# Transfers with more distance in the attention, maxima sent by ScalarE, and another order of row differences at the joint, in a transformer block on one core

## Chip, core and metric

The kernel runs on one core of one Trainium2 chip, in one launch. The metric is the device time of that launch in microseconds (us); lower is better. The engines are TensorE (PE; its weight loads are PEld), VectorE (DVE), ScalarE (ACT), GpSimd (POOL) and SyncE (SP), whose only work here is to issue DMA transfers, one after the other.

## What is computed

One transformer block of 2048 rows and width 512, modulated by a condition vector. The attention has 32 heads of 16 and four segments of 512 rows: causal attention inside a segment, mixed by a gate with a read of a memory of the segments before. A dense layer with gelu follows.

```python
h = _layernorm(x) * (1 + ca) + sa
x = x + ga * attention(h)              # 32 heads, 4 segments of 512 rows
h = _layernorm(x) * (1 + cb) + sb
x = x + gb * (gelu(h @ w1 + b1) @ w2 + b2)

# attention, for one segment s
p = softmax(qs @ ks.T * scale + causal_mask)
a_mem = (phi(qs) @ M) / (phi(qs) @ z + 1e-6)
o = g * a_mem + (1 - g) * (p @ vs)     # then o @ wo
M, z = M + phi(ks).T @ vs, z + phi(ks).sum(rows)
```

## The kernel before

There are four stages. The first (0 to about 200 us) projects q, k and v of all segments and reads the memory. The attention follows (about 200 to 486 us). Then comes the dense layer: its first product in fourteen "quads" (`quad`), which combine two row halves and two column halves with seven products in place of eight, each of them from high and low parts in three matmuls, and its second product (`ffn2`). The joint is the passage from the attention to the first quads.

**The attention.** P counts pairs of heads (0 to 63), Q groups of four heads of one segment (0 to 31), U groups of eight (0 to 15). For each Q, `load_stacks` loads a stack of q and one of k (qst, kst; four buffers of each), which hold each value as several bf16 terms in 96 rows. `s_part` (places S) computes the logits with rows on partitions only to take their maxima: `masked_max` (L613) does that with the causal mask on VectorE; for the two narrower blocks TensorE adds the mask as a product (L645) and one `tensor_reduce` takes the maxima of two heads (L617). `m_rows` (L661, GpSimd) splits the maxima into three bf16 terms, `m_put` turns them by a product (L667) and ScalarE copies them to a tile ms, and `m_send` (L675) stores them as rows 96 to 98 of the q stack. `st_part` (places T) then computes the logits transposed, with the maxima already subtracted (L693); ScalarE takes the exponential (L708, L719), and GpSimd's `affine_select` (L696) clears what is above the diagonal. `pv_part` (L733) multiplies by the values and a column of ones, which gives the denominators.

After that a U goes through memory: `pv_out` copies the result (ScalarE), `pv_store` stores it to TD (L751), `pv_in` loads the denominators dn and the values opk (L756, L758), the memory's share amB (L765) and for the last segment its divisor rm (L770, multiplied by `mem_mix`, L800). `den` inverts dn (VectorE, GpSimd), `den_store` stores it to RD (L784), `rb_in` loads it back spread over the rows, rbB (L788). `mix` multiplies and adds (L793, L795; GpSimd for U under 13), and `o_hi` (ScalarE) and `o_lo` make high and low parts. `wo_part` (L821) projects them, `wo_out` adds the rows of x, and `wo_store` stores the result to X2D (L847). Of the finished segments `ln2_load` loads the rows xt back (L556), `ln2_stats`, `ln2_rstd` and `ln2_apply` (L568; GpSimd for segment 0) normalise them, and `ln2_turn` (L574, L576) transposes them for the dense layer.

**What sets the order.** The order on each engine is written out by hand. `ap(place, f, ...)` puts a step at a place; one Q is 20 places, so Q's own products run at 20 Q to 20 Q + 20. ORDER says where among a step's S and T parts the places c0 to c19 lie. The dictionary PRM holds the distances: `dnl` (pv_in behind the last PV product), `den`, `rbl` (rb_in behind den), `rdl` (den_store behind den), `mix`, `ohi`, `olo` relative to 40 U; `mrows`, `mput`, `msl` for the maxima; `ln` and `ht` for the segments' normalisation and transposes. A transfer issued by SP waits in its turn for everything that it needs, and those behind it wait with it. At the joint, what is still left of the places is called by name with `rest(U, ...)`. There `r_sub` builds the row differences t1 to t4 from the transposed rows hr, `r_hi` (ScalarE) and `r_lo` (VectorE) make their high and low parts, and `w_hi` and `w_lo` those of w1. In the quads `bg(n, i, f, ...)` puts a background step into part i of quad n; `g_out` (L1085) applies gelu to a part and stores it (GD, L1086); `ln2_load3` loads the rows of segment 3.

Of the kernel before, what the change touches and what calls it, by code (L numbers as in the profile page):

```python
# [33 lines left out]
 'den': [84, 84, 84, 84],  # L34
 'dnl': 11,
 'rbl': 12,
 'rdl': 4,
 'tsl': 4,
 'msl': 2,
 'xol': 6,  # L40
 'mix': 107,
 'ohi': 117,
 'olo': 119,
 'end': {'rbl': 7, 'mix': 103, 'ohi': 111, 'olo': 116},
 'wo': [[20 * i + o for i in range(8) for o in (2, 5)]] * 2 + [[20 * i + o for i in range(4) for o in (2, 5, 8, 14)]],
 'wox': -25,
 'olate': 16,
 'mixu': 13,
 'olou': 13,
 'ht': [493, 503, 513, 523],  # L50
 'ht1': 644,
 'ln': [[400, 413, 449, 454], [531, 566, 603, 624]],
 'lnl': [0, 4, 20, 34],
# [23 lines left out]
 'mmix': 88,  # L77
 'lnd': [[11, 10], [10, 2]],
# [3 lines left out]
 'm': [0, 0, 0, 1],  # L82
# [19 lines left out]
def block_kernel(ctx: ExitStack, tc: tile.TileContext, x, wq, wk, wv, wo, betaq, betam,  # L102
                 w1, b1c, w2, b2, ccol, wmod, maskbd, mask8, out):
    nc = tc.nc
    v, act, pool, pe, sp = nc.vector, nc.scalar, nc.gpsimd, nc.tensor, nc.sync
# [57 lines left out]
    NK = 4  # L163
# [420 lines left out]
    with ExitStack() as pb:  # L584
# [89 lines left out]
        def m_send(Q):  # L674
            sp.dma_start(qst[Q % NK][96:99], mss.pop(Q))  # L675
# [255 lines left out]
        def ap(pos, f, *a):  # L931
            at(pos // 10, pos % 10, f, *a)
# [20 lines left out]
        for U in range(16):  # L953
            z = U // 4
            ap(40 * U + 20 + PRM["pv"][3][0] + PRM["dnl"], pv_in, U)
            if U == 15:
                ap(40 * U + 20 + PRM["pv"][3][0] + PRM["dnl"], am_in, U)
            p = {**PRM, **PRM["end"]} if U > 13 else PRM
            den_at = 40 * U + PRM["den"][z]
            ap(den_at, den, U)  # L960
            if U < 14:
                ap(den_at + PRM["rdl"], den_store, U)
            ap(den_at + p["rbl"] + (5 if U == 14 else 0), rb_in, U)
            assert 20 + PRM["pv"][3][0] + PRM["dnl"] <= PRM["den"][z] and PRM["den"][z] + p["rbl"] <= p["mix"]
            ap(40 * U + PRM["mmix"], mem_mix, U)
            ap(40 * U + p["mix"], mix, U)
            assert PRM["mmix"] <= p["mix"]
            late_by = PRM["olate"] if U in (6, 10) else 0
            ap(40 * U + p["ohi"] + late_by, o_hi, U)
            ap(40 * U + p["olo"] + late_by, o_lo, U)  # L970
            assert PRM["den"][z] <= p["mix"] <= p["ohi"] <= p["olo"]
# [12 lines left out]
        for i, (ln, ld) in enumerate(zip(PRM["ln"], PRM["lnd"])):  # L984
            assert ln[0] + PRM["lnl"][3] * i > 160 * i + 241 + PRM["wo"][i][15] and ln[1] > ln[0]
            assert ln[1] + 3 * ld[0] < ln[2] < ln[3] and ln[3] + 3 * ld[1] < (PRM["ht"][0], PRM["ht1"])[i]
        assert PRM["ln"][1][0] > PRM["ht"][3] and PRM["ht"] == sorted(PRM["ht"])
# [9 lines left out]
        for i, (ln, ld) in enumerate(zip(PRM["ln"], PRM["lnd"])):  # L997
# [43 lines left out]
    with ExitStack() as pc:  # L1041
# [134 lines left out]
        rest(15, "mem_mix")  # L1176
        r_lo(0, "t1")
        r_lo(0, "t2")
# [52 lines left out]
        bg(2, 1, ln2_load3)  # L1231
# [196 lines left out]
```

## Time and profile before

| | |
|---|---|
| median of 3 runs | 810.78 us (809.48 to 811.25) |
| profiled execution, its own time | 808.31 us |
| its span, first to last instruction | 806.6 us |
| busy: PE, DVE, ACT, POOL | 778.6, 553.5, 476.2, 331.8 us |
| mean granted TensorE clock | 0.992 |
| moved by DMA | 156.09 MB, mean 194 GB/s |

Times within the profile are microseconds from the first instruction. An entry of the timeline reads: start, duration, engine, line, operation, output tile, input tiles, shapes, count, and in brackets the idle time of the engine before it with what ended it. "SPq" and "ACTq" are the queues in which an engine issues its transfers. An entry of the waits reads: who waits, for whom, us in total, number of times, longest. Matmuls are pipelined, so from one to the next the starts count and not the durations.

### The profile page before, as it was taken

To read this page: it belongs to the slowest core of one execution; us is meant where nothing else is said; L and a number is where in the kernel's file an instruction comes from. 1 tells how busy PE (TensorE), PEld (TensorE's weight loads), DVE (VectorE), ACT (ScalarE), POOL (GpSimd) and SP (SyncE) were. 2 spreads that over 40 slices of the span, in tenths; PEclk is the share of its full clock that TensorE was granted. 3 is DMA by queue.
4 is the path that set the end of the run, shared out by engine and by line. 5 is a ranking of instruction groups with operands and counts; after the bars stand their busy time and mean duration, and the time that the engine had idled before them with its cause. 6 is when DMAs were issued, how large, how long until landed. Compare 5 with 4: busy or idle time off the path is not lost.

```text
span 806.6 us, 14065 instructions
## 1 busy us (share of the span) xinstructions
PE 778.6 (97%) x4631; PEld 539.2 (67%) x4631; DVE 553.5 (69%) x1275; ACT 476.2 (59%) x910; POOL 331.8 (41%) x554
## 2 busy tenths in 40 slices
PE   8999999999999999998989798989999999999998
PEld 4877767876545455554545455768888888888887
DVE  6686697458888877876867687867668866632523
ACT  4465545465888877775777475757745336653221
POOL 1347266451578655565875485133000404400000
PEclk9999999999999999999999999899999999999999
DMA  9596857395555667767657764585575744445443
GB/s 338 179 320 230 277 181 238 142 328 175 169 165 164 189 191 197 194 174 224 173 173 200 196 175 135 166 266 170 203 252 165 221 135 154 161 143 165 157 136 117
DMA packets 108817, 156.09 MB, mean 194 GB/s; under 512 B 16324, under 2 KB 55620, under 8 KB 108744
## 3 DMA queue, kind: packets, MB, share of 16 engines
q1 hardware_dynamic: 107880, 153.63, 60.9%
q10 hardware_dynamic: 864, 1.57, 0.5%
q8 instruction: 36, 0.59, 0.3%
q14 instruction: 37, 0.30, 0.1%
HBM read 93.95 MB, written 60.83 MB: 192 GB/s over the span
## 4 chain that ended last, share of the span: by engine, by line
PE 74%; DMA 7%; DVE 6%; ACT 4%; POOL 4%; issue 3%; SPq 1%; ACTq 0%; DVEq 0%; POOLq 0%
PE bx L1080 8%; PE att L693 7%; PE pv L733 7%; PE q L313 5%; PE bx L1345 5%; PE att L606 5%; PE by L1345 4%; PE bv L1345 4%; PE k L313 4%; PE bv L1080 4%; PE mm L821 3%; PE v L464 3%; PE spare L1345 2%; PE by L1080 2%; DMA qst<-ms 2%
## 5 line engine op out<-in xcount | busy, mean ns | idle before, releaser
L613 DVE CUSTOM_DVE_ANT_0 dump<-att,maskb 128x512 bf16<-128x512 f32 (+1 forms) x292 | 159.4, 595 | 44.6 <-PE att L606 22.0
L708 ACT ACTIVATE pt<-att 128x384 f32<-128x384 f32 (+1 forms) x256 | 124.8, 544 | 24.6 <-PE att L693 21.2
L696 POOL TENSOR_SCALAR_AFFINE_SELECT pt<-pt 128x256 f32<-128x256 f32 x256 | 103.2, 421 | 74.3 <-ACT pt L708 59.3
L693 PE MATMUL att<-qst,kst 99*128 99x256 bf16 (+3 forms) x512 | 108.3, 302 | 7.6 <-DMA qst<-ms 5.7
L693 PEld LDWEIGHTS <-kst 99*128 99x128 bf16 x512 | 43.8, 98 | 71.8 <-issue 35.9
L865 POOL TENSOR_TENSOR wb<-wa 128x256 f32<-128x256 f32 x24 | 21.4, 894 | 154.9 <-DMA wa<-in_w 144.3
L606 PE MATMUL att<-kst,qst 96*128 96x512 bf16 (+1 forms) x292 | 76.5, 344 | 3.9 <-DMA qst<-QD 3.3
L733 PE MATMUL pv<-pt,V 128*32 128x512 f32 (+1 forms) x992 | 79.6, 439 | 0.0
L719 ACT ACTIVATE pt<-att 128x256 f32<-128x256 f32 (+1 forms) x128 | 62.7, 493 | 23.2 <-PE att L693 22.7
L617 DVE TENSOR_REDUCE nm<-att 128x2 f32<-128x256 f32 (+1 forms) x110 | 56.4, 534 | 15.0 <-PE att L645 11.6
L136 DVE TENSOR_TENSOR gl<-s,gh 128x512 fp32r<-128x512 f32 x34 | 23.7, 697 | 42.1 <-ACT gh L133 42.1
L733 PEld LDWEIGHTS pv<-pt,V 128*32 128x32 f32 x992 | 25.9, 109 | 36.2 <-issue 28.1
L133 ACT ACTIVATE gh<-s 128x512 fp32r<-128x512 f32 x34 | 21.3, 628 | 46.3 <-PE spare L1345 16.7
L1085 ACT ACTIVATE s<-s,b1t 128x512 f32<-128x512 f32 x42 | 30.2, 720 | 17.9 <-DVE s L1089 17.9
L1089 DVE TENSOR_TENSOR s<-bv,s 128x512 f32<-128x512 f32 x28 | 19.2, 687 | 24.4 <-PE bv L1080 19.0
L606 PEld LDWEIGHTS <-qst 96*128 96x128 bf16 x292 | 23.7, 98 | 13.6 <-issue 7.6
L509 POOL TENSOR_TENSOR q<-qr,q 128x512 bf16<-128x512 f32 x16 | 18.7, 1168 | 27.8 <-ACT q L508 27.5
L645 PE MATMUL att<-maskb,identb 128*128 128x256 bf16 x110 | 29.9, 278 | 0.0
L500 POOL TENSOR_SCALAR qp<-qp 128x512 f32<-128x512 f32 x12 | 18.8, 1563 | 25.8 <-ACT qp L495 25.8
L136 DVE TENSOR_TENSOR w1ml<-s,w1mh 128x512 fp32r<-128x512 f32 x18 | 13.0, 721 | 22.5 <-ACT w1mh L133 22.5
L643 PE MATMUL att<-kst,qst 96*128 96x128 bf16 (+1 forms) x110 | 27.3, 248 | 0.8 <-ACT pt L708 0.8
L133 ACT ACTIVATE w1mh<-s 128x512 fp32r<-128x512 f32 x18 | 11.3, 629 | 26.8 <-PE spare L1345 11.3
(364 smaller groups left out, 2152.0 us busy)
## 6 DMA issues: line engine op xcount, KB each, us to landing
GD<-s SPq DMA_DIRECT2D x56, 256.0 KB
s<-GD SPq DMA_DIRECT2D x52, 256.0 KB
kst<-KD SPq DMA_DIRECT2D x32, 384.0 KB
qst<-QD SPq DMA_DIRECT2D x32, 384.0 KB
TD<-ts SPq DMA_DIRECT2D x32, 256.0 KB
xt<-X2D SPq DMA_DIRECT2D x28, 256.0 KB
wa<-in_w SPq DMA_DIRECT2D x28, 256.0 KB
QD<-q SPq DMA_DIRECT2D x16, 384.0 KB
```

Of the source, the lines that this page charges most:

```text
L136: lo_eng.tensor_tensor(out=lo, in0=src, in1=hi.bitcast(F32), op=ALU.subtract)
L313: pe.matmul(ps, a[:, k, 128 * g:128 * g + 128], b[k], start=(k == 0 and i == 0), stop=(k == KB - 1 and i == 2))
L606: pe.matmul(ps, q_of(P, h, i), k_of(P, h, 128 * (i + 1)), start=True, stop=True)
L613: v.tensor_tensor_reduce(out=dump[n_dump[0] % 2][:, :n], in0=src, in1=maskb[:, 512 - n:], scale=-1.0, scalar=-4 * NEG, op0=ALU.add, op1=AL ...
L617: v.tensor_reduce(out=dst, in_=src, axis=AX.X, op=ALU.max, negate=True)
L693: pe.matmul(ps, k[:99, e, 128 * j:128 * j + 128], q[:99, e, 128 * j:512], start=True, stop=True)
L696: pool.affine_select(out=t, in_=t, pattern=pattern, compare_op=ALU.is_ge, fill=0.0, base=0, channel_multiplier=-1)
L708: act.activation(pt[:, h, :], ps[:, :n], AF.Exp, scale=0.25)
L719: act.activation(pt, pv_, AF.Exp, scale=0.25)
L733: pe.matmul(ps[32 * c:32 * c + 32, lo:hi], V[4 * s + j][:, VW * hd:VW * hd + 32], pt[:, c % 2, lo - o:hi - o], start=start, stop=stop)
L1080: pe.matmul(ps, a[:, i, k, :], b[k], start=start and k == 0 and c == 0, stop=k == 1 and c == 2, skip_group_check=not start)
L1345: pe.matmul(ps, a[:, c], w[:, lo:hi], start=(f == 0 and i == 0), stop=(last and i == 2))
```

## The change

- In the attention the places of `pv_in`, `den`, `rb_in`, `mix`, `o_hi` and `o_lo` are later for U 0 to 10 and 12; U 11 and 13 ("quick") keep the old ones, 14 and 15 ("end") too. `mem_mix` of U 12 goes from 88 to 100. The delay of the high and low parts of U 6 and 10 (`olate`) is dropped.
- `m_send` of Q 10 to 31 is issued by ScalarE's queue in place of SP's.
- From Q 14 on, one more of the narrow maxima (first pair of the Q, 256 columns) is taken with the mask on VectorE, so its mask product goes.
- The loads, statistics and applications of segments 0 and 1 have places of their own; the transposes of segment 0 move from 493, 503, 513 to 498, 506, 514.
- At the joint all row differences are VectorE's, and the order of differences, high and low parts and the last denominators is another.
- The rows of segment 3 are loaded in part 2 of quad 3 in place of part 1 of quad 2.

```diff
--- before.py
+++ after.py
@@ -31,26 +31,27 @@
  'mrows': -21,
  'mput': -13,
  'stacks': -65,
- 'den': [84, 84, 84, 84],
- 'dnl': 11,
- 'rbl': 12,
+ 'den': 92,
+ 'dnl': 18,
+ 'rbl': 18,
  'rdl': 4,
  'tsl': 4,
  'msl': 2,
+ 'msa': 10,
  'xol': 6,
- 'mix': 107,
- 'ohi': 117,
- 'olo': 119,
- 'end': {'rbl': 7, 'mix': 103, 'ohi': 111, 'olo': 116},
+ 'mix': 120,
+ 'ohi': 130,
+ 'olo': 132,
+ 'quick': {'dnl': 11, 'den': 84, 'rbl': 12, 'mix': 107, 'ohi': 117, 'olo': 119},
+ 'end': {'dnl': 11, 'den': 84, 'rbl': 7, 'mix': 103, 'ohi': 111, 'olo': 116},
  'wo': [[20 * i + o for i in range(8) for o in (2, 5)]] * 2 + [[20 * i + o for i in range(4) for o in (2, 5, 8, 14)]],
  'wox': -25,
- 'olate': 16,
  'mixu': 13,
  'olou': 13,
- 'ht': [493, 503, 513, 523],
+ 'ht': [498, 506, 514, 523],
  'ht1': 644,
- 'ln': [[400, 413, 449, 454], [531, 566, 603, 624]],
- 'lnl': [0, 4, 20, 34],
+ 'ln': [{'in': [388, 397, 408, 417], 'stat': [420, 427, 434, 446], 'rstd': 449, 'on': [460, 467, 481, 487]},
+        {'in': [528, 537, 548, 568], 'stat': [566, 576, 586, 596], 'rstd': 603, 'on': [624, 626, 628, 630]}],
  'wl': [26, 66, 80, 81],
  'gate': 197,
  'vb': [1, 0, 1, 0],
@@ -74,12 +75,11 @@
  're': 'v',
  'am3': 1,
  'rme': 'p',
- 'mmix': 88,
- 'lnd': [[11, 10], [10, 2]],
+ 'mmix': 100,
  'mp': 0,
  'wout': ['vvvv', 'vava', 'vvvv'],
  'dens': ['p', 'p', 'p', 'v'],
- 'm': [0, 0, 0, 1],
+ 'm': [0, 1, 0, 1],
  'mq': 14,
  'pvo': ['a', 'a'],
  'mse': 'a',
@@ -672,7 +672,7 @@
         mss = {}
 
         def m_send(Q):
-            sp.dma_start(qst[Q % NK][96:99], mss.pop(Q))
+            (sp if Q < PRM["msa"] else act).dma_start(qst[Q % NK][96:99], mss.pop(Q))
 
         pts = {}
         late = []
@@ -952,23 +952,22 @@
                 ap(20 * Q + pvo + PRM["tsl"], pv_store, Q)
         for U in range(16):
             z = U // 4
-            ap(40 * U + 20 + PRM["pv"][3][0] + PRM["dnl"], pv_in, U)
+            p = {**PRM, **(PRM["end"] if U > 13 else PRM["quick"] if U in (11, 13) else {})}
+            in_at, den_at = 40 * U + 20 + PRM["pv"][3][0] + p["dnl"], 40 * U + p["den"]
+            ap(in_at, pv_in, U)
             if U == 15:
-                ap(40 * U + 20 + PRM["pv"][3][0] + PRM["dnl"], am_in, U)
-            p = {**PRM, **PRM["end"]} if U > 13 else PRM
-            den_at = 40 * U + PRM["den"][z]
+                ap(in_at, am_in, U)
             ap(den_at, den, U)
             if U < 14:
                 ap(den_at + PRM["rdl"], den_store, U)
             ap(den_at + p["rbl"] + (5 if U == 14 else 0), rb_in, U)
-            assert 20 + PRM["pv"][3][0] + PRM["dnl"] <= PRM["den"][z] and PRM["den"][z] + p["rbl"] <= p["mix"]
-            ap(40 * U + PRM["mmix"], mem_mix, U)
+            assert in_at <= den_at and p["den"] + p["rbl"] <= p["mix"]
+            mm_at = 88 if p["mix"] < 120 else PRM["mmix"]
+            ap(40 * U + mm_at, mem_mix, U)
             ap(40 * U + p["mix"], mix, U)
-            assert PRM["mmix"] <= p["mix"]
-            late_by = PRM["olate"] if U in (6, 10) else 0
-            ap(40 * U + p["ohi"] + late_by, o_hi, U)
-            ap(40 * U + p["olo"] + late_by, o_lo, U)
-            assert PRM["den"][z] <= p["mix"] <= p["ohi"] <= p["olo"]
+            assert mm_at <= p["mix"] <= p["ohi"] <= p["olo"]
+            ap(40 * U + p["ohi"], o_hi, U)
+            ap(40 * U + p["olo"], o_lo, U)
         for s in range(NSEG - 1):
             for b in range(4):
                 w = [160 * s + 240 + i for i in PRM["wo"][s][4 * b:4 * b + 4]]
...
@@ -994,12 +994,12 @@
         at(-1, 9, swap)
 
         ap(PRM["gate"], gate_load)
-        for i, (ln, ld) in enumerate(zip(PRM["ln"], PRM["lnd"])):
+        for i, ln in enumerate(PRM["ln"]):
             for b in range(4):
-                ap(ln[0] + PRM["lnl"][b] * i, ln2_load, i, b)
-                ap(ln[1] + ld[0] * b, ln2_stats, i, b)
-                ap(ln[3] + ld[1] * b, ln2_apply, i, b, (pool, v)[i])
-            ap(ln[2], ln2_rstd, i)
+                ap(ln["in"][b], ln2_load, i, b)
+                ap(ln["stat"][b], ln2_stats, i, b)
+                ap(ln["on"][b], ln2_apply, i, b, (pool, v)[i])
+            ap(ln["rstd"], ln2_rstd, i)
         for j in range(2):
             for i in range(4):
                 ap(PRM["wsub"][j] + i, w_sub, j, i, v)
@@ -1161,21 +1161,21 @@
         rest(15, "pv_in", "am_in")
         for b in range(4):
             wo_seg(3, b, range(2))
-        for i in range(2):
-            w_hi(0, i)
-        w_lo(0, 0)
+        w_hi(0, 0)
         r_sub(0, "t1")
         r_hi(0, "t1")
+        w_lo(0, 0)
         r_sub(0, "t2")
+        w_hi(0, 1)
+        r_lo(0, "t1")
         r_hi(0, "t2")
         w_lo(0, 1)
         rest(15, "den", "rb_in")
         rest(14, "mem_mix")
+        r_lo(0, "t2")
+        rest(15, "mem_mix")
         for n in ("t3", "t4"):
-            r_sub(0, n, pool)
-        rest(15, "mem_mix")
-        r_lo(0, "t1")
-        r_lo(0, "t2")
+            r_sub(0, n)
         rest(14, "mix")
         for b in range(4):
             wo_x(3, b)
@@ -1228,7 +1228,7 @@
             for b in range(lo, hi):
                 ln2_apply(s, b, v)
 
-        bg(2, 1, ln2_load3)
+        bg(3, 2, ln2_load3)
         for s, n in ((2, 2), (3, 4)):
             for b in range(4):
                 bg(n, 1 + b, ln2_stats, s, b)
```

More of the change, by code (lines that the diff above doesn't have):

```diff
@@ L983, in block_kernel @@
         assert PRM["wl"] == sorted(PRM["wl"]) and PRM["gate"] > PRM["wl"][1] + 60
-        for i, (ln, ld) in enumerate(zip(PRM["ln"], PRM["lnd"])):
-            assert ln[0] + PRM["lnl"][3] * i > 160 * i + 241 + PRM["wo"][i][15] and ln[1] > ln[0]
-            assert ln[1] + 3 * ld[0] < ln[2] < ln[3] and ln[3] + 3 * ld[1] < (PRM["ht"][0], PRM["ht1"])[i]
-        assert PRM["ln"][1][0] > PRM["ht"][3] and PRM["ht"] == sorted(PRM["ht"])
+        for i, ln in enumerate(PRM["ln"]):
+            assert all(a > 160 * i + 242 + PRM["wo"][i][4 * b + 3] + PRM["xol"] and a < c < ln["rstd"]
+                       for b, (a, c) in enumerate(zip(ln["in"], ln["stat"])))
+            assert ln["rstd"] < ln["on"][0] and ln["on"][3] < (PRM["ht"][0], PRM["ht1"])[i]
+        assert PRM["ln"][1]["in"][0] > PRM["ht"][3] and PRM["ht"] == sorted(PRM["ht"])
         def gate_load():
@@ L996, in block_kernel @@
         ap(PRM["gate"], gate_load)
-        for i, (ln, ld) in enumerate(zip(PRM["ln"], PRM["lnd"])):
+        for i, ln in enumerate(PRM["ln"]):
             for b in range(4):
-                ap(ln[0] + PRM["lnl"][b] * i, ln2_load, i, b)
-                ap(ln[1] + ld[0] * b, ln2_stats, i, b)
-                ap(ln[3] + ld[1] * b, ln2_apply, i, b, (pool, v)[i])
-            ap(ln[2], ln2_rstd, i)
+                ap(ln["in"][b], ln2_load, i, b)
+                ap(ln["stat"][b], ln2_stats, i, b)
+                ap(ln["on"][b], ln2_apply, i, b, (pool, v)[i])
+            ap(ln["rstd"], ln2_rstd, i)
         for j in range(2):
```

## The prediction

> **What bounds the kernel now.** I read the page first, then TensorE's waits, then the chain of waits, then the queue of SP beside the engine that feeds it.
>
> ```profile
> span 806.6 us, 14065 instructions
> ...
> PE 778.6 (97%) x4631; PEld 539.2 (67%) x4631; DVE 553.5 (69%) x1275; ACT 476.2 (59%) x910; POOL 331.8 (41%) x554
> ...
> PEclk9999999999999999999999999899999999999999
> ```
>
> TensorE is busy for 97% of the span, so it is the bound, and idle TensorE is worth at most 28 us; but a stage in which it runs slowly also counts as busy. The stretches tell more (PE, PEld, DVE, ACT, POOL busy us with instruction counts, granted clock, DMA share, GB/s):
>
> ```profile
> 340.00:360.00 20.00, 20.00 (x168) 10.13 (x166) 16.66 (x58) 15.70 (x34) 11.48 (x26) 1.00 0.72 202
> 440.00:460.00 20.00, 15.12 (x120) 7.77 (x119) 13.18 (x42) 10.61 (x23) 10.56 (x21) 0.96 0.59 168
> 500.00:520.00 20.00, 17.82 (x62) 13.27 (x63) 16.66 (x26) 10.84 (x19) 6.20 (x6) 0.83 0.37 125
> ```
>
> A clean stretch of the attention issues 168 matmuls, the stretch at 440 only 120. At 500, the joint, the clock is down to 0.83. Who is waited for:
>
> ```profile
> PE att L693 <- DMA qst<-ms: 5.7, 3, 2.8
> PE att L606 <- DMA qst<-QD: 3.3, 2, 2.7
> ```
>
> The row maxima (ms) and the stacks reach SBUF late. The chain of waits has, once in each step (one Q), the first eight PV products; the distance between two of them is the length of a step:
>
> ```profile
> 262.38 0.99 PE pv L733 x8
> 270.08 1.00 PE pv L733 x8
> 287.01 0.99 PE pv L733 x8
> ...
> 358.43 0.99 PE pv L733 x8
> 367.26 1.00 PE pv L733 x8
> ...
> 370.14 4.99 DMA qst<-ms
> ...
> 381.27 1.00 PE pv L733 x8
> ...
> 465.33 0.99 PE pv L733 x8
> ```
>
> Clean steps take 7.70 (262.38 to 270.08) early and 8.83 (358.43 to 367.26) later, where the output projection runs beside. One schedule place is a twentieth, 0.44 us. Against that there are three losses. (A) 270.08 to 287.01 is two steps in 16.93 instead of 15.40: 1.5 lost. (B) 367.26 to 381.27 is one step in 14.01: 5.2 lost. (C) 381.27 to 465.33 is eight steps in 84.06, where eight clean ones are 70.6; sixteen transposes and up to twelve more projection products, about 4 us by the 0.23 per product below, belong there too: 9.4 lost. Sum of A to C: 16.1.
>
> What makes B and most of C is seen by laying ScalarE's copy of ms beside SP's queue:
>
> ```profile
> 366.42 0.27 ACT L127 ACTIVATE ms<-pv 48x128 bf16<-48x128 f32 x1
> ...
> 447.47 0.27 ACT L127 ACTIVATE ms<-pv 48x128 bf16<-48x128 f32 x1
> ```
>
> ```profile
> 364.40 4.30 SPq L556 DMA_DIRECT2D xt<-X2D  x4
> ...
> 370.14 0.78 SPq L675 DMA_DIRECT2D qst<-ms  x1
> ...
> 443.63 0.61 SPq L756 DMA_DIRECT2D dn<-TD  x1
> ...
> 447.08 0.43 SPq L175 DMA_DIRECT2D kst<-KD  x1
> ...
> 454.65 0.78 SPq L675 DMA_DIRECT2D qst<-ms  x1
> ```
>
> The maxima are ready at 366.69 and 447.74 and leave at 370.14 and 454.65, 3.5 and 6.9 us later. SP issues in order, and ahead of them stand transfers that wait for others to land: the four row loads of segment 0, all at place 400 behind the store of place 392, and the denominator's load, seven places behind its store. The stacks at 447.08 (place 555) stood behind that same load (place 549).
>
> **The change part by part.**
>
> *Sends of maxima from ScalarE (Q from 10).* All 22 leave SP, and none waits any longer for a denominator or a row load. This takes A and B, of which I count 1.4 and 5.0. The price is on ScalarE:
>
> ```profile
> L675 SPq DMA_DIRECT2D qst<-ms x32: 729/785/832, 193.3 to 473.0; - x32
> ```
>
> An issue holds its queue 0.785 us; 22 of them are 17.3 us of ScalarE if nothing hides them, and nothing if its idle time does. The stretch at 340 shows 15.70 of 20 busy, so 1.9 idle per 8.83 step, more than one issue. Behind the send on ScalarE are the exps of parts T1 and T4; behind those GpSimd's causal masks, the PV products and the six att banks. The kernel before shows no send there, so the ends stay 0 and 17.3; I take 2.5, near the hidden end, since the idle row is for the stage in which 19 of the 22 lie. The early three, without projection work beside, pay most.
>
> On SP the transfers behind an old send gain its wait. [...]
>
> *More distance.* Per U the store of TD to the load of dn goes from 7 to 14 places (3.1 to 6.2 us), the store of RD to the load of rbB from 8 to 14 (3.5 to 6.2); rbB to mix goes from 11 to 10 (4.9 to 4.4). The loads dn, opk, amB (and rm) now stand one place behind the stacks instead of six ahead, so a late TD no longer holds the stacks. The four row loads stand at 388, 397, 408, 417, the last 25 places behind the store. GpSimd has the other half of C:
>
> ```profile
> 405.39 2.08 POOL L568 TENSOR_SCALAR xt<-xt,cmv,crs 128x512 f32<-128x512 f32 x1
> ...
> 408.36 0.23 PE L667 MATMUL pv<-identb,nm 128*128 128x128 bf16 x1 [1.17 <-POOL nm L661]
> ...
> POOL opk L793 <- DMA rbB<-RD: 17.4, 10, 2.9
> ```
>
> The normalisation of segment 0 (four at 2.08) and the mix delay the split of the maxima (L661), and TensorE waits 1.17. The new places put both behind that split (459, 479) instead of just ahead; the total work stays, so the last of the four ends close to its transposes (place 498), and I leave 1.5 there. GpSimd's wait for rbB (1.74 each) can grow by the 0.4 that mix comes closer; as the exact delay of U=10 decides what U=11 finds (second rival), I leave 2.9 more. Of C's 9.4 I take 5.0; ends 0 and 9.4.
>
> *Masked maximum (m, 18 Q from 14).* One mask product goes, two products keep their width:
>
> ```profile
> 363.47 0.27 PE L645 MATMUL att<-maskb,identb 128*128 128x256 bf16 x1
> 363.50 0.47 PE L821 MATMUL mm<-woh,oh 128*128 128x512 f32 x1
> 363.81 0.39 PE L821 MATMUL mm<-woh,ol 128*128 128x512 f32 x1
> 364.04 0.40 PE L821 MATMUL mm<-wol,oh 128*128 128x512 f32 x1
> ```
>
> A product of 512 takes 0.23 (363.81 to 364.04); mask and product together take 0.34 (363.47 to 363.81), so the mask 0.11; 18 are 2.0. VectorE, 16.66 of 20 busy in the clean stretch, does two maxima of 256 for one of 512; it has the room. I take 1.4; ends 0 and 2.0.
>
> *Joint.*
>
> ```profile
> 498.72 0.39 PE L1080 MATMUL bv<-rt1h,w1mh 128*128 128x512 f32 x1
> ...
> 511.21 0.40 PE L1080 MATMUL bx<-rt3h,w1mh 128*128 128x512 f32 x1
> ```
>
> ```profile
> 494.74 3.48 DVE L886 TENSOR_TENSOR s<-hr,hr 128x512 f32<-128x512 f32 x2
> ...
> 503.56 1.28 DVE L899 TENSOR_TENSOR rt2l<-s,rt2h 128x512 fp32r<-128x512 f32 x2
> ```
>
> ```profile
> 494.37 0.58 SPq L756 DMA_DIRECT2D dn<-TD  x1
> ```
>
> Between these products stand 24 of 0.23, 5.5 us; they take 12.5, so 7.0 are lost, to low parts of t1 that come late and to the clock. VectorE's pair of differences takes 3.48 beside GpSimd's differences and 1.28 alone. With all four pairs on VectorE, the first one ahead of the wait for w1, t1's low parts are ready near 495, before TensorE asks at 498.7. What is late next: VectorE meets the denominator of U=15, whose load leaves at 494.37 and is there between 495.0, when its issue ends, and 499.4, if it takes the 4.99 of the ms at 370.14; I take 497. Behind it come t2's low parts (1.3), t3 and t4 (2.6), the mix of U=14 (1.3): 502.2, with half a pair (0.6) for the denominator itself 502.8, and 0.6 for the high part. TensorE, done with t2 at 501.5, waits about 2 us. That gives 4.7; if that wait again lowers the clock, 1.9. I take 3.0; ends -1 (VectorE's 2.6 uncovered behind a later denominator) and 7.0. [...]
>
> *Segment 3's rows a quad later.*
>
> ```profile
> 542.01 0.50 PE L1080 MATMUL bx<-rt2h,w1mh 128*128 128x512 f32 x1 [1.54 <-ACT s L1116]
> ...
> 541.36 0.60 ACT L1116 ACTIVATE s<-bx 128x512 f32<-128x512 f32 x1 [4.26 <-DMA GD<-s]
> ...
> 532.90 1.87 SPq L556 DMA_DIRECT2D x<-X2D  x4
> ```
>
> Four loads of 256 KB stand just ahead of the stores that ScalarE waits for, and TensorE waits 1.54. Behind the stores of quad 3 they meet a statistic one step-group later, some 8 us ahead of it. I take 1.2; ends -1 (VectorE waiting for the rows) and 1.5.
>
> **Sum.** 1.4 + 5.0 + 5.0 + 1.4 - 2.5 + 3.0 + 1.2 = 14.5. The profiled execution took 808.31, so 793.8; the median of the runs, 810.78, lies 2.5 above it: **796.3**, own range 788 to 802.
>
> **Rivals.**
>
> *ScalarE is held by its sends: slower.* A transfer also waits for an older one that it shares no data with:
>
> ```profile
> SPq L1086 <- DMA wa<-in_w: 0.9, 1, 0.9
> ```
>
> By the order of the issues I take that one to be the eighth back, which no row states. For five odd Q (15 to 25) it is rbB, 19 places (8.4 us) earlier. Before, rbB is there 4.9 + 1.74 = 6.6 us after its place, so 1.8 us are spare. If the denominators make rbB later than 8.4, ScalarE stands with its exps behind it, GpSimd gets its work later, and the next denominator is later still. With the longest such wait (2.9) at each of the five and all issues uncovered (17.3 instead of 2.5) the loss is 29.3; three quarters of it, 22, give 808.3 - 14.5 + 22 + 2.5 = 818. Against it: SP is freed of the very waits that made rbB late. It decides from 14.5 us of further ScalarE time on TensorE's path. Chance 0.11.
>
> *GpSimd hands a delay on.* U=10's mix (520) now stands just ahead of U=11's denominator (524), and U=11 keeps the old distances. Late by one rbB wait, U=11's own chain of store, load and mix is late too, ScalarE's high part waits, and C returns 4 us; if the joint's new wait lowers the clock, 3.0 go too. 14.5 - 7 gives 803.3 in the median. For it: the rbB row; against: POOL's 11.48 of 20 in the clean stretch, time to catch up. Chance 0.20.
>
> *The transfers are late anyway.* If landing and not the issue made ms late, A to C stay (-11.4): 807.7, or no change with the sends dearer. B's 4.99 from issue to landing would be its sign; the waits before the issue speak against it. Chance 0.09, 0.05 of it within 0.2%.
>
> **How the numbers follow.** The forecast has 0.60. Faster by over 0.2%, which is about what measurements of this kernel can tell (809.2 and below), is 0.60 + 0.20 + 0.04 = 0.84; same 0.05; slower 0.11. The range reaches from 787, my sum with C and the joint nearer their full size, through both faster rivals to 809; it leaves out the slow case and a little at the bottom.
>
> **What would show it.** Right: no TensorE wait for ms from 270 on, chain steps of 8.7 from 330 to 440, ScalarE's queue with 22 issues of 0.7 to 0.8; mask products down from 110 to 92; in the joint VectorE's pairs at 1.3 and one wait ahead of the projection of U=14. Wrong: exps that start after a send with TensorE waiting for pt; GpSimd idle over 3 us at U=11's mix; a stretch at 500 still at 0.83. I am wrong if A to C shrink and the time doesn't.

## Result and the profile after

The change makes the kernel faster: 801.3 us in the median of 4 runs (797.24 to 802.42) against 810.13 (807.83 to 811.25, 4 runs); ratio 0.9896, interval 0.9866 to 0.9927. That is 8.8 us where I forecast 14.5, at 796.3; the time lies inside the range. The profiled execution took 800.94, 7.4 less than that of before. Three executions among all the runs of this document took far longer than the rest (1089, 1548 and 1969 us); all medians and ratios here leave them out, and as the one of 1089 is the profiled one of the run called "attention alone", nothing is read from its trace.

The page of the kernel after (span, busy time, granted clock by slices):

```profile
span 799.2 us, 14063 instructions
...
PE 778.2 (97%) x4613; PEld 536.1 (67%) x4613; DVE 553.0 (69%) x1333; ACT 474.4 (59%) x910; POOL 324.0 (41%) x550
...
PEclk9999999999999999999999999999999999999999
```

TensorE's busy time hardly moved (778.6 to 778.2); its idle time went from 28.0 to 21.0, which is the gain. The stretches of the kernel after:

```profile
440.00:460.00 20.00, 18.63 (x144) 10.21 (x133) 16.09 (x58) 12.81 (x28) 11.60 (x27) 1.00 0.72 206
460.00:480.00 20.00, 15.67 (x116) 7.54 (x114) 16.54 (x32) 11.50 (x26) 14.27 (x21) 0.92 0.56 148
500.00:520.00 20.00, 18.19 (x74) 13.03 (x73) 15.92 (x26) 14.27 (x26) 4.86 (x5) 1.00 0.54 168
```

440 to 460 went from 120 matmuls to 144, and 500 to 520 from a clock of 0.83 to 1.00. But 460 to 480 now has 116 matmuls at 0.92: a new loss at the end of the attention.

To see where the time went I cut the trace at the first PV product of a step, as the prediction did. In both kernels the attention lies between the first logits and segment 1's transposes; the first two rows are of before, the other two of after:

```profile
197.32 0.65 PE L693 MATMUL att<-qst,kst 99*128 99x384 bf16 x3
486.24 1.97 PE L574 MATMUL att<-ident,xt 128*128 128x128 f32 x16
```

```profile
196.52 0.65 PE L693 MATMUL att<-qst,kst 99*128 99x384 bf16 x3
485.13 1.97 PE L574 MATMUL att<-ident,xt 128*128 128x128 f32 x16
```

| part of the trace | before | after | gained | forecast |
|---|---|---|---|---|
| first stage, to the first logits | 197.32 | 196.52 | 0.8 | 0 |
| steps to Q 8 | 72.69 | 72.68 | 0.0 | 0 |
| A, two steps | 16.93 | 16.43 | 0.5 | 1.4 |
| nine steps between A and B | 80.25 | 79.60 | 0.65 | mask and sends |
| B, one step | 14.02 | 10.65 | 3.4 | 5.0 |
| C, eight steps | 84.06 | 81.48 | 2.6 | 5.0 |
| end of the attention | 20.99 | 27.76 | **-6.8** | 0 |
| joint, transposes to t3 | 24.97 | 19.96 | 5.0 | 3.0 |
| t3 to the end | 295.4 | 294.1 | 1.3 | 1.2 |

The gains in A to C are smaller than forecast, and the end of the attention takes nearly all of them back: in this pair the attention gains 0.3 us. These are single executions. The run "joint and rows alone" below has the attention of before, and its trace takes 291.1 us for it where before takes 288.9, so a part of this table is uncertain by some 2 us; the first stage, which the change leaves as it was, shows 0.8. The chain of waits of the kernel after names the places:

```profile
338.92 1.00 PE pv L733 x8
347.65 0.99 PE pv L733 x8
356.57 0.99 PE pv L733 x8
364.82 6.68 DMA qst<-ms
375.95 0.99 PE pv L733 x8
...
444.53 7.75 DMA qst<-ms
458.62 7.92 DMA rbB<-RD
466.68 1.29 POOL opk L793
```

Clean steps alternate 8.73 and 8.92. The maxima (ms) are on the chain again, now with a long time from issue to landing. The timeline shows that the issue itself is on time:

```profile
364.46 0.27 ACT L127 ACTIVATE ms<-pv 48x128 bf16<-48x128 f32 x1
364.82 0.73 ACTq L675 DMA_DIRECT2D qst<-ms  x1
371.55 0.66 PE L693 MATMUL att<-qst,kst 99*128 99x384 bf16 x3 [1.56 <-DMA qst<-ms]
...
444.53 0.73 ACTq L675 DMA_DIRECT2D qst<-ms  x1
452.32 0.66 PE L693 MATMUL att<-qst,kst 99*128 99x384 bf16 x3 [1.34 <-DMA qst<-ms]
```

The new loss at the end belongs to U 12. Its rbB leaves behind the four loads of U 13 (places 589 and 590), lands after 8 us, and everything of U 12 comes late on GpSimd, with TensorE waiting for its masked exps:

```profile
457.92 0.59 SPq L770 DMA_DIRECT2D rm<-rdd  x1
458.62 0.57 SPq L788 DMA_DIRECT2D rbB<-RD  x1
...
466.68 1.28 POOL L793 TENSOR_TENSOR opk<-opk,rbB 128x512 f32<-128x512 f32 x1 [4.31 <-DMA rbB<-RD]
...
474.97 1.05 PE L733 MATMUL pv<-pt,V 128*32 128x512 f32 x4 [1.28 <-POOL pt L696]
...
479.07 1.92 PE L733 MATMUL pv<-pt,V 128*32 128x512 f32 x4 [3.05 <-POOL pt L696]
```

These two waits of TensorE are 4.3 us of the 6.8; in the same stretch the granted clock is 0.92.

A smaller new wait stands in the step from 423.67 (12.41 us long): U 10's rbB is late for GpSimd, the high part of U 10 is late on ScalarE, and the exps are behind it:

```profile
424.23 1.27 POOL L793 TENSOR_TENSOR opk<-opk,rbB 128x512 f32<-128x512 f32 x1 [4.87 <-DMA rbB<-RD]
...
426.87 0.63 ACT L127 ACTIVATE oh<-opk 128x512 fp32r<-128x512 f32 x1 [1.75 <-POOL opk L795]
...
427.83 0.59 PE L693 MATMUL att<-qst,kst 99*128 99x512 bf16 x2 [1.89 <-ACT pt L719]
```

The joint after has its pairs of differences at 1.3 us, no wait inside t1 and t2, and two short ones ahead of the projection of U 14:

```profile
491.31 1.29 DVE L886 TENSOR_TENSOR s<-hr,hr 128x512 f32<-128x512 f32 x2
...
501.03 0.49 PE L821 MATMUL bv<-woh,oh 128*128 128x512 f32 x1 [0.53 <-ACT oh L127]
502.45 0.50 PE L821 MATMUL bv<-woh,ol 128*128 128x512 f32 x1 [0.93 <-DVE ol L810]
...
505.08 0.39 PE L1080 MATMUL bx<-rt3h,w1mh 128*128 128x512 f32 x1
```

In the quads the wait of 1.54 (at 542.01 before) is gone, and so is one of 1.40 ahead of it (at 534.71); one of 0.95, ended by the same ScalarE addition, stands a quad earlier (at 525.55), where before has none.

### The profile page after: what moved, and what is told of

Read it like the earlier page. It is cut to its first block, busy times and chain, and to the rows that moved or that the text cites. A ratio compares the mean times of both kernels' runs of the same rounds, so it can differ in the third digit from the quotient of the medians.

```text
span 799.2 us, 14063 instructions
## 1 busy us (share of the span) xinstructions
PE 778.2 (97%) x4613; PEld 536.1 (67%) x4613; DVE 553.0 (69%) x1333; ACT 474.4 (59%) x910; POOL 324.0 (41%) x550
## 4 chain that ended last, share of the span: by engine, by line
PE 75%; DMA 6%; POOL 6%; DVE 5%; ACT 4%; issue 3%; SPq 0%; ACTq 0%; DVEq 0%; POOLq 0%
PE bx L1080 8%; PE pv L733 6%; PE att L693 6%; PE q L313 5%; PE bx L1345 5%; PE att L606 5%; PE by L1345 5%; PE bv L1345 5%; PE bv L1080 4%; PE k L313 4%; PE mm L821 3%; PE v L464 3%; DMA qst<-ms 3%; PE spare L1345 2%; PE by L1080 2%
## 5 line engine op out<-in xcount | busy, mean ns | idle before, releaser
L613 DVE CUSTOM_DVE_ANT_0 dump<-att,maskb 128x384 bf16<-128x384 f32 (+2 forms) x328 | 172.6, 575 | 49.9 <-PE att L606 22.9
L708 ACT ACTIVATE pt<-att 128x384 f32<-128x384 f32 (+1 forms) x256 | 127.2, 546 | 23.5 <-PE att L693 15.2
L733 PE MATMUL pv<-pt,V 128*32 128x512 f32 (+1 forms) x992 | 82.3, 444 | 4.4 <-POOL pt L696 4.3
L606 PE MATMUL att<-kst,qst 96*128 96x384 bf16 (+2 forms) x328 | 83.7, 337 | 1.3 <-DVE nm L613 0.6
L865 POOL TENSOR_TENSOR wb<-wa 128x256 f32<-128x256 f32 x24 | 23.1, 962 | 149.4 <-DMA wa<-in_w 125.5
L719 ACT ACTIVATE pt<-att 128x256 f32<-128x256 f32 (+1 forms) x128 | 60.6, 494 | 20.8 <-PE att L693 20.2
L133 ACT ACTIVATE gh<-s 128x512 fp32r<-128x512 f32 x34 | 21.3, 628 | 46.3 <-PE spare L1345 16.9
L617 DVE TENSOR_REDUCE nm<-att 128x2 f32<-128x256 f32 (+1 forms) x92 | 43.9, 503 | 3.6 <-PE att L645 2.8
L606 PEld LDWEIGHTS <-qst 96*128 96x128 bf16 x328 | 27.3, 98 | 13.7 <-issue 9.7
L127 ACT ACTIVATE ts<-pv 128x512 f32<-128x512 f32 x31 | 18.5, 597 | 17.3 <-PE pv L733 17.3
L613 DVE DVE_READ_ACCUMULATOR2_ANT nm<- 128x1 f32 x328 | 27.2, 83 | 0.0
```

What stands on the lines that cost most here:

```text
L606: pe.matmul(ps, q_of(P, h, i), k_of(P, h, 128 * (i + 1)), start=True, stop=True)
L613: v.tensor_tensor_reduce(out=dump[n_dump[0] % 2][:, :n], in0=src, in1=maskb[:, 512 - n:], scale=-1.0, scalar=-4 * NEG, op0=ALU.add, op1=AL ...
L617: v.tensor_reduce(out=dst, in_=src, axis=AX.X, op=ALU.max, negate=True)
L708: act.activation(pt[:, h, :], ps[:, :n], AF.Exp, scale=0.25)
L719: act.activation(pt, pv_, AF.Exp, scale=0.25)
L733: pe.matmul(ps[32 * c:32 * c + 32, lo:hi], V[4 * s + j][:, VW * hd:VW * hd + 32], pt[:, c % 2, lo - o:hi - o], start=start, stop=stop)
```

## The experiments

Each was run against the kernel before on the same chip; the table gives the ratio, and the length of the end of the attention (27.76 after, 20.99 before) in the profiled execution.

| run | median us | ratio to before, interval | end of attention |
|---|---|---|---|
| the change | 801.30 | 0.9896 (0.9866 to 0.9927) | 27.76 |
| joint and rows alone | 804.75 | 0.9960 (0.9938 to 0.9982) | 20.37 |
| attention alone | 806.16 | 0.9981 (0.9954 to 1.0008) | not used |
| all sends by SP | 799.34 | 0.9886 (0.9848 to 0.9924) | 29.61 |
| old distances | 799.43 | 0.9886 (0.9847 to 0.9926) | 21.79 |
| mask back | 803.28 | 0.9927 (0.9903 to 0.9952) | 27.60 |
| t3, t4 on GpSimd | 802.63 | 0.9917 (0.9894 to 0.9941) | 27.45 |
| maxima four places earlier | 800.37 | 0.9918 (0.9888 to 0.9948) | 29.33 |
| U 12 quick | 796.77 | 0.9860 (0.9815 to 0.9905) | 22.31 |
| U 12 quick, sends by SP | 797.57 | 0.9855 (0.9825 to 0.9885) | 21.29 |
| U 12 quick, last sends by SP | 797.85 | 0.9864 (0.9836 to 0.9892) | 24.97 |
| U 12 quick, its loads at 556 | 794.95 | 0.9833 (0.9798 to 0.9868) | 20.99 |
| the same, rows of segment 1 later | 798.09 | 0.9878 (0.9839 to 0.9918) | 26.32 |

**Which part brings the time.** Joint and rows alone, on the kernel before (the joint's order is that of the change; here are its differences and the rows):

```diff
-        for n in ("t3", "t4"):
-            r_sub(0, n, pool)
...
+        for n in ("t3", "t4"):
+            r_sub(0, n)
...
-        bg(2, 1, ln2_load3)
+        bg(3, 2, ln2_load3)
```

> The kernel before with only the joint's new order and segment 3's rows a quad later; the attention is the old one. Theory (the whole gain lies behind the attention: by the two traces 5.0 us from the first product of t1 to the first of t3 and what is near it, and 1.3 us in the quads): 6.3 us faster than before, ratio about 0.992, the chain's step at 367 still 14 us long. Rival (the joint is only better because the new attention leaves other transfers and engines in front of it): 2 us or less, and low parts of t1 late again.

Measured: 3.2 us faster, between the two expectations; its joint takes 20.94 (24.97 before). Attention alone is the kernel after with these lines undone:

> The kernel after with the old joint (two differences on GpSimd, the old order) and segment 3's rows at their old quad: the attention's part of the change alone (distances, the mask of the odd steps' second block, sends by ScalarE). The joint and the rows alone brought 3.2 us of the 8.4 that the whole change brings by the ratio to the kernel before. Theory (attention's part brings the rest, 4 to 6 us in the median, and the 0.3 us between the two profiled executions is a chance pair: single executions of one kernel differ by up to 3 us in attention): ratio 0.992 to 0.995. Rival (attention brought nothing, the parts only work together): ratio 0.998 to 1.001.

Measured: 1.5 us faster (interval from 3.7 faster to 0.6 slower). The ratio, 0.9981, is inside the rival's 0.998 to 1.001: alone, the attention's part is not shown to bring anything. The two parts give 4.7, the whole 8.4. The difference of 3.7 us is no larger than the intervals of the three added as independent errors, also about 3.7 us, so whether the parts help each other stays open. What is settled is that the attention's part alone brings at most 3.7 of the 10.3 us that my sum gave it (1.4, 5.0, 5.0 and 1.4, less 2.5); which of the two parts brings more is not.

**Is it the sends or the distances?** All sends back to SP, then all U back to the old distances (with the old delay of U 6 and 10):

```diff
- 'msa': 10,
+ 'msa': 99,
```

> The changed kernel with all sends of maxima back on SP. Theory (the sends by ScalarE bring back about 5 us of waits at Q 11, 20 and 28 and cost about 2 to 3 beside the high parts): 2 to 4 us slower than the changed kernel, ratio to before 0.993 to 0.995, with waits for ms of over 2 us. Rival (ScalarE's sends cost as much as they bring, since the maxima land as late from one queue as from the other): the same as the changed kernel or up to 2 us faster, even steps 8.7 instead of 8.9.

```diff
-            p = {**PRM, **(PRM["end"] if U > 13 else PRM["quick"] if U in (11, 13) else {})}
+            p = {**PRM, **(PRM["end"] if U > 13 else PRM["quick"] if U < 14 else {})}
```

> The changed kernel with the old distances for every U (with the old delay of the high and low parts of U 6 and 10); sends by ScalarE, mask, segment places and joint stay new. Theory (the later places make the waits at U 10's mix, 3.5 us, and at U 12's mix, about 6 us with the clock): 5 to 9 us faster than the changed kernel, 792 to 796, ratio to before 0.978 to 0.983. Rival (the distances earn what they cost, since the denominators would again hold SP and with it the stacks): within 2 us of the changed kernel, or slower.

Both miss the theory, and the time is as both rivals have it: each is as fast as the kernel after, within the intervals. With sends by SP the nine steps between A and B take 78.55 instead of 79.60, so the sends cost ScalarE's side 1.05 there; and B takes 8.88, with the maxima leaving 0.03 us behind their copy. SP is not always in time: the maxima of Q 27 leave 6.15 us late, behind a denominator's store. With the old distances the end of the attention is back at 21.79, and other waits are there: B takes 12.54, and TensorE waits 3.7 us for exps at two places. Both runs keep the row loads' new places, and no run has these alone, so how much of the gain at B belongs to them, to the distances and to the sends stays open; the sends by ScalarE are not needed for it.

**The end of the attention.** U 12 joins the U with short distances:

```diff
-            p = {**PRM, **(PRM["end"] if U > 13 else PRM["quick"] if U in (11, 13) else {})}
+            p = {**PRM, **(PRM["end"] if U > 13 else PRM["quick"] if U in (11, 12, 13) else {})}
```

> The changed kernel with U 12 alone on the old distances. Theory (rbB of U 12 is issued right behind the four loads of U 13 and lands 8 us later; GpSimd's mix waits 4.3 for it, and the masks behind it hold TensorE 4.3 with the clock at 0.92): that wait goes, 5 us faster than the changed kernel, about 796, ratio to before 0.983. Rival (GpSimd has too much to do there whatever the order: reciprocal root, mix, two multiplications by rm, low part): TensorE waits as long for the masks, and the time is within 1 us of the changed kernel's.

Measured: ratio 0.9860, about 3 us below the change by the ratios and 4.5 by the medians; the trace's attention takes 281.98 (288.61), its end 22.31. By time alone the intervals of the two ratios overlap; the traces carry the theory. The end takes 27.45 to 29.61 in the five traces with long distances for U 12, and 20.37 to 24.97 in the seven with short ones, the last run of the table apart, whose end has another cause (below). Its C keeps a loss of another kind. Timeline of this run:

```profile
436.37 0.60 SPq L770 DMA_DIRECT2D rm<-rdd  x1
...
438.80 0.27 ACT L127 ACTIVATE ms<-pv 48x128 bf16<-48x128 f32 x1
...
442.28 0.73 ACTq L675 DMA_DIRECT2D qst<-ms  x1
442.34 1.26 POOL L800 TENSOR_TENSOR amB<-amB,rm 128x512 f32<-128x512 f32 x1 [2.38 <-DMA rm<-rdd]
443.35 0.60 ACT L708 ACTIVATE pt<-att 128x512 f32<-128x512 f32 x1 [3.73 <-issue]
443.99 0.38 PE L693 MATMUL att<-qst,kst 99*128 99x256 bf16 x2 [2.11 <-ACT pt L708]
```

The maxima are ready at 439.07 and the send leaves at 442.28, just when rm has landed (GpSimd, which needs rm, starts at 442.34). It shares no data with rm. ScalarE stands for 3.73, and TensorE waits 2.11 for the exps behind. In the run with old distances the waits name the pair themselves:

```profile
ACT pt L708 <- DMA rm<-rdd: 4.4, 1, 4.4
```

That is the first rival's mechanism, at another transfer than the one I named. Why it is rm, no view says. In the prediction I took such a transfer, by the order of the issues, to be the eighth back, and that is my estimate here too: in one queue, as in the second of the runs below, rm is the eighth before the send; here the row load of 443.54 leaves behind the send, and rm is the seventh by time. Three runs test it: all sends by SP, the last three sends by SP, and U 12's loads left at place 556, so that by this count it is no longer rm:

```diff
- 'msa': 10,
+ 'msa': 99,
```

> The kernel after with U=12 and U=13 and U=11 on the quick distances (as in the run before, median 796.8 us) and all 32 sends of maxima issued by SP. Theory (ScalarE is held by its sends, in step 28 by 3.7 us, and the even steps each lose 0.19 us beside o_hi): the 3.7 us and about 9 x 0.19 = 1.7 us go, less what the maxima come late again behind SP's queue (1 to 3 us): 2 to 4 us below the run before, about 793 to 795 us. Rival (the sends on SP wait for the same earlier transfer, the maxima come late by the same time and TensorE waits for ms instead): within 1 us of 796.8, and the wait in step 28 or 29 is then ended by ms.

```diff
-            (sp if Q < PRM["msa"] else act).dma_start(qst[Q % NK][96:99], mss.pop(Q))
+            (sp if Q < PRM["msa"] or Q > 28 else act).dma_start(qst[Q % NK][96:99], mss.pop(Q))
```

> The kernel after with U=11, U=12 and U=13 on the quick distances and the sends of Q=10 to Q=28 by ScalarE, those of Q=29, 30 and 31 by SP. Theory (the send of Q=29 waits on ScalarE for the broadcast of rm, an earlier transfer that it shares no data with, and the exps behind it on ScalarE wait too): ScalarE's gap of 3.7 us in step 28 goes and the step falls from 14.2 us by 2 to 3 us: about 794 us. Rival (rm's landing itself holds the step, through the mix or through the lateness of ms): the step stays above 13 us and the time within 1 us of 796.8.

```diff
+            if U == 12:
+                p["dnl"] = 18
...
-            mm_at = 88 if p["mix"] < 120 else PRM["mmix"]
+            mm_at = 96 if U == 12 else 88 if p["mix"] < 120 else PRM["mmix"]
```

> The kernel after with U=11, U=12 and U=13 on the quick distances, sends by ScalarE, but U=12's loads left at place 556 (not 549) and its product with the gate's rows at place 576: the transfer eight ahead of the send of Q=29 is then the small load of den's rows and not the broadcast rm. Nothing else moves. Theory (the send of Q=29 held ScalarE until the eighth transfer before it had landed, and that was rm): ScalarE's gap of 3.7 us in step 28 goes, step 28 falls from 14.2 us to about 11.5, and the kernel is 2 to 3 us faster than with all three quick (ratio 0.986), about 0.983. Rival (the send waited for something else, or the time comes back in the mix of U=12, whose loads land 3 us later): ratio 0.985 to 0.988.

The first two miss the theory and stay within 1.1 us of 796.8: off ScalarE the same send is late on SP (4.8 and 3.0 us behind its copy). In the second of them SP's queue reads

```profile
443.54 0.71 SPq L784 DMA_DIRECT2D RD<-dn  x1
446.69 0.32 SPq L556 DMA_DIRECT2D xt<-X2D  x1
447.10 0.81 SPq L675 DMA_DIRECT2D qst<-ms  x1
```

with the maxima ready at 444.11: SP waits for a store that the row load needs, and the send stands behind; rm, the eighth issue before it, is itself there only at 446.44, when GpSimd starts with it. The third does what it should at that place: the send leaves at 444.08, 0.03 us after its copy (443.78, 0.27 long), ScalarE's wait of 3.7 is gone, and from the first transposed logits of Q 28 to those of Q 29 it takes 11.77 instead of 14.23 (rm, sent at 438.59, is the fifth issue before it there). It has the lowest time of all kernels here, 794.95, ratio 0.9833, below the change and the kernel before. That ratio is inside the interval of the run that it mends, so these two can't be told apart by time, and C, 82.71 against 82.31, shows no gain. Another wait is there instead, 3.35 us for the maxima of Q 28, just ahead of the stretch that got shorter:

```profile
430.47 0.73 ACTq L675 DMA_DIRECT2D qst<-ms  x1
...
438.62 0.66 PE L693 MATMUL att<-qst,kst 99*128 99x384 bf16 x3 [3.35 <-DMA qst<-ms]
```

**Why the maxima land late.** Maxima four places earlier, on the kernel after:

```diff
- 'mput': -13,
+ 'mput': -17,
```

> The kernel after with the products and the sends of the maxima four places (about 1.75 us) earlier in every step; the GpSimd work that they need ends 3.1 us ahead of the product now. Theory (the maxima that come late, 1.6 us at Q=21 and 1.3 us at Q=29 in the profiled execution, come late because they are landed 6.7 and 7.7 us after an issue that is on time; four places earlier covers it): TensorE's waits for ms go, 2 to 3 us faster than the kernel after, ratio about 0.987. Rival (the landing is set by the burst of the transfers around it, so an earlier issue lands at the same time, or the product holds TensorE): within 1 us of the kernel after.

The rival held by the medians, 0.9 us apart; by the ratios this run is 1.8 us slower, with overlapping intervals, and no gain either way. The timeline of this run, and its stretch, then the kernel after's (DMA share and GB/s are the last columns):

```profile
362.68 0.73 ACTq L675 DMA_DIRECT2D qst<-ms  x1
...
370.92 0.66 PE L693 MATMUL att<-qst,kst 99*128 99x384 bf16 x3 [1.99 <-DMA qst<-ms]
```

```profile
365.00:372.00 7.00, 5.01 (x49) 2.43 (x44) 4.74 (x20) 4.23 (x9) 3.92 (x9) 1.00 0.89 250
```

```profile
365.00:372.00 7.00, 5.41 (x50) 2.08 (x49) 5.52 (x21) 4.44 (x10) 4.22 (x10) 1.00 0.89 269
```

The step starts at 364.37 in this run and at 365.23 in the kernel after. Counted from there, these 12 KB are sent 1.3 us earlier, take 8.2 us instead of 6.7 and are used 0.2 later. The DMA engines are 0.89 busy in both stretches, so I took it that the landing goes by what is queued there. In the run with U 12's loads at 556 they are 0.97 busy from 430 to 440, so the last run takes row loads out of that stretch:

```diff
-        {'in': [528, 537, 548, 568], 'stat': [566, 576, 586, 596], 'rstd': 603, 'on': [624, 626, 628, 630]}],
+        {'in': [528, 550, 568, 576], 'stat': [566, 576, 586, 596], 'rstd': 603, 'on': [624, 626, 628, 630]}],
```

> The kernel of the run before last (quick distances for U=11 to 13, U=12's loads at place 556; ratio 0.983) with three of the four row loads of segment 1 for the second layer norm later: at places 528, 550, 568 and 576 instead of 528, 537, 548 and 568. In that kernel's trace the 16 DMA engines are 0.97 busy from 430 to 440 us, the maxima of Q=28 are issued in time at 430.5 and land 8.1 us later, and TensorE waits 3.35 us for them. Theory (the landing is set by what shares the DMA engines in that stretch): with two loads of 256 KB out of it the maxima of Q=28 land about 2 us earlier, TensorE's wait falls to about 1.5 us or less, and the kernel is 1.5 to 2.5 us faster, ratio about 0.981. Rival (the load is not what delays them, or the bytes come back as a later wait of the steps 29 and 30): ratio 0.983 or above.

```profile
439.02 0.66 PE L693 MATMUL att<-qst,kst 99*128 99x384 bf16 x3 [0.77 <-DMA qst<-ms]
...
462.50 0.45 SPq L765 DMA_DIRECT2D amB<-AMD  x1
...
464.05 0.26 ACT L127 ACTIVATE ms<-pv 48x128 bf16<-48x128 f32 x1
...
467.70 0.73 ACTq L675 DMA_DIRECT2D qst<-ms  x1
...
473.18 0.66 PE L693 MATMUL att<-qst,kst 99*128 99x384 bf16 x3 [3.99 <-DMA qst<-ms]
```

The wait for Q 28 fell from 3.35 to 0.77, its landing from 8.1 to 5.6 us, and C to 79.83 from 82.71, as the theory has it, though the DMA engines are still 0.95 busy from that send to its landing. But the maxima of Q 31 are now 3.99 late, the end takes 26.32 instead of 20.99, and the ratio is 0.9878 instead of 0.9833, with overlapping intervals. The time is the rival's; how the wait comes back is another matter. The maxima of Q 31 are ready at 464.31 and leave at 467.70, 3.4 us late, and then land in 5.5. What they wait for, no view names: ScalarE's next exps are put down to TensorE. Counted by the issues amB, the load sent by SP at 462.50, is the eighth before this send, so by my estimate it is held once more, and by amB. That load is late itself. It stands behind the load of den's rows, which waits 7.8 us in SP's queue for the store to TD (5.8 in the run that this one builds on), and that store left 2.6 us behind the moved row load of 450.20. So the moved bytes may have come back by way of this store; no run has the store without the row load, so it is not shown.

**Sizes of two terms.** The mask of the first pair's 256 columns, from Q 14 on, back on TensorE, and t3 and t4 of the joint back on GpSimd in the new order:

```diff
- 'm': [0, 1, 0, 1],
+ 'm': [0, 0, 0, 1],
```

> The kernel after (801.3 us) with the mask of the odd steps' second block back where it was, the 18 products of it on TensorE again. Theory (each product costs TensorE its own 0.11 us, nothing waits on GpSimd or VectorE for the mask): 18 x 0.11 = 2.0 us slower, and clean odd steps at 8.83 us instead of 8.72. Rival (the products lie in time in which TensorE waits anyway): within 0.5 us of the kernel after.

```diff
-            r_sub(0, n)
+            r_sub(0, n, pool)
```

> The kernel after (801.3 us) with the differences of t3 and t4 at the joint back on GpSimd, in the new order of the joint. Theory (the engine is what counts: a pair of differences takes GpSimd 3.5 us beside VectorE's work and VectorE 1.3): the products of t3 start 2 to 3.5 us later and the kernel is 2 to 3.5 us slower, 803.3 to 804.8. Rival (the order is what counts, GpSimd's differences are ready before TensorE asks): within 0.8 us of the kernel after.

Without the mask edit the kernel is 2.5 us slower by the ratios, whose intervals overlap; in the trace each of the nine steps is longer, clean odd ones 8.84 instead of 8.73, even ones 9.03 instead of 8.92, the nine 80.57 instead of 79.60. That is 0.11 for each product, as the theory has it. With GpSimd the kernel is 1.7 us slower, between the two expectations, and the intervals of both ratios overlap. Its trace shows where: TensorE reaches t3's first product early (18.0 us behind the transposes, 19.96 in the kernel after) and waits behind it.

```profile
500.54 3.42 POOL L886 TENSOR_TENSOR hr<-hr,s 128x512 f32<-128x512 f32 x2
...
501.20 0.50 PE L1080 MATMUL bx<-rt3l,w1mh 128*128 128x512 f32 x1 [0.40 <-DVE rt3l L899]
...
502.89 0.50 PE L1080 MATMUL bx<-rt3l,w1mh 128*128 128x512 f32 x1 [0.74 <-DVE rt3l L899]
```

From the transposes to the end of the kernel it takes 315.8 (after 314.1, before 320.4). That would give the order and the rows 4.6 of the 6.3 and VectorE 1.7; but the eleven traces with VectorE's differences in the new order spread from 312.7 to 316.5, so VectorE's share is not shown.

## Why the prediction was right, and where it was not

**Direction.** Right, and for a part of the reasons: in before, the queue of SP held the maxima; the joint lost time to late low parts; and the rows' wait went.

**A and B (6.4 forecast, 3.9 measured).** The wait ahead of the issue went as forecast; TensorE's did not, because the sum had no term for a longer landing: 6.68 us at B where before shows 4.99. The third rival, with 0.09, was right for this half. It is not so in every execution: of the six traces with the same schedule up to there, B takes 8.90 to 9.04 in three, which is the whole 5.0 that I forecast, and 10.40 to 10.70 in the others. The two runs with all sends by SP differ in the same way, 8.88 and 10.48, and there a landing of 7.63 is seen (the send at 443.16). What was left at B with ScalarE's queue is 6.68 us from issue to landing, and with sends by SP the kernel is as fast (0.9886 against 0.9896, within the intervals). The 3.5 and 6.9 us that the old queue held the maxima back fell to 0.03 and 0.80 with sends by SP and the new distances, and to 1.65 and 4.11 with sends by ScalarE and the old distances.

**C and the second rival.** I looked for a handed-on delay at U 10 and U 11. U 10's was there (12.41 us in the step from 423.67), but the dear one is two U later: U 12 keeps long distances, U 13 behind it has short ones, so U 12's rbB is issued behind U 13's loads. I followed the places of U 10 and U 11 only. This is the step that failed: the sum had no term for the end of the attention, and it is -6.8.

**Mask and sends.** Mask: 0.97 in nine steps, one product each, which makes 1.9 for the eighteen. I took 1.4; the 2.0 of its rows was right. Sends: 1.05 in the same nine steps, and 0.33 in the step from 269.20, against 2.5 for all 22: about right as far as it can be read, hidden in idle time but for the even steps, in which ScalarE has a high part beside.

**First rival.** Not in the kernel after, where no send leaves more than 0.4 us behind its copy. Late sends show in four variants: old distances (1.65 and 4.11 us late), U 12 quick (3.21), maxima earlier (2.41) and the last run (1.41 and 3.40). For two of them the traces put ScalarE's wait down to an older transfer: rm for the 4.11, a row load for the 1.41; the 3.21 ends as rm lands, and for the other three it is not shown. That a send holds ScalarE in this way was right, the transfer wrong, and TensorE waited 2 to 4 us where I had priced 22. That the older one is the eighth back stays my estimate.

**Joint and rows.** Forecast 3.0 and 1.2, in the profiled pair 5.0 and 1.3. The 5.0 is at the high end: in eleven traces with this joint it takes 19.5 to 23.0 us, 21.3 in the mean, where before's one trace has 24.97, so 3.0 is within what they show. The wait that I feared ahead of U 14's projection is 0.53 and 0.93 instead of 2, and the clock stayed at 1.00. The stretch from 460 has 0.92 with waits of 1.28 and 3.05, and the joint before had 0.83 with none longer than 1.26, so the longest wait alone does not tell what the clock does here.

**The total.** The change brought 8.8 us of the 14.5, and 7.4 in the profiled pair: 0.3 in the attention, where the sum had 10.3, 6.3 behind it, where it had 4.2, and 0.8 in the first stage, which the change doesn't touch. That the time is still inside the range is in part luck: the term that was left out (-6.8) and the 4.9 us missing in A to C are met by a joint at the high end and by terms that nobody forecast.

## To carry to other kernels

When steps of several groups get different distances, write the issue queue out in order at each place where a long one meets a short one: a group with long distances followed by one with short ones puts its last load behind the other's bulk (here rbB of U 12, 7.92 us from issue to landing). A late small transfer has two parts, before its issue and behind it, and they are to be read apart: the first was mended here by another place (3.21 us to 0.03 for the maxima of Q 29), the second became shorter when row loads left the stretch (8.1 us to 5.6 for those of Q 28), and an earlier issue did not help it (6.7 to 8.2 in the step of B). After a transfer is moved, look again for sends that leave late: in the last run the maxima of Q 31 left 3.4 us behind their copy, and 0.25 in the run that it builds on. Distances are worth setting one group at a time: changing one group (U 12) and then the places of its loads took the kernel from 0.9896 to 0.9833 of the time before, though neither step alone is clear of the noise.

## What the runs showed that I had not expected

- A transfer was held while one that it shares no data with was under way from another queue: with U 12 quick the send of 12 KB on ScalarE stood 3.2 us, until rm, sent by SP 5.9 us earlier, had landed, and all of ScalarE's arithmetic stood behind it.
- A transfer of 12 KB took 6.7 to 8.2 us in stretches in which the DMA engines were 0.85 to 1.00 busy, but 5.0 (at 370.14 before) and 5.6 (Q 28 in the last run) in others no less busy than 0.95, so the busy share alone does not tell it. Sent 1.3 us earlier in its step, it was used no earlier.
- The granted clock fell to 0.92 in a stretch whose longest wait of TensorE was 3.05 us.
